# A recurrence with routed experts: a block reordered, transposed keys moved into A's PSUM banks, routing spread over four blocks

## Chip, cores and metric

The kernel runs on 1 core of one Trainium2 chip. The metric is device time in microseconds (us) of that core. Engines are named as in the profile: PE (TensorE; its weight loads are PEld), DVE (VectorE), ACT (ScalarE), POOL (GpSimd) and SP (SyncE, which here only issues DMAs).

## What is computed

The reference is a linear recurrence over time for 4 batches and 8 heads of width 48, and a top-1 mixture of experts behind it:

```
for t in range(768):                                   # per batch and head
    cur   = outer(u * k[t], v[t])
    y[t]  = r[t] @ (state + cur)
    state = w[t][:, None] * state + outer(k[t], v[t])
x = y as 3072 tokens of 384
logits = x @ w_gate; e = argmax(logits); gate = softmax(logits)[e]
out = gate * (relu(x @ w1[e]) @ w2[e])                 # 8 experts, 384 -> 1024 -> 384
```

## The kernel before

**Recurrence.** Time is cut into 24 blocks n = 0..23 (12 chunks of 64 steps, two batch pairs), so blocks n and n+2 belong to one recurrence and n%2 says which. For a block the kernel makes, on DVE, running products of w from the front (`pre`, L322, with the reciprocal of their ends, L325) and from the back (`suf`, L331); kh = k * suf on DVE (`dve_kh`, L339); rh = r * pre and rk = r * k on POOL (`pool_rh` L364, `pool_rk` L358). On PE: the transposed keys (`pe_kt`, four transposes, L465), the 64 by 64 products A = kh x rh (`pe_a`, 32 matmuls, L418), the part of the output that comes from the state (`pe_inter`, 32 matmuls, L435), the part inside the block (`pe_av`, 32 matmuls, L444), the new state U (`pe_dp`, 32 matmuls, L456), the u-coefficients (`pe_c`, 16 matmuls, L476) and the transposed output xT (`pe_xT`, 3 transposes, L484). ACT copies PSUM to SBUF: kt (L396), g from U (L377), ct (L382), xr from yp (L404), xT (L409); it also writes the diagonals of the matrix `at`, eight activations a block (`act_diag`, L390), and two small paddings (`act_pad` L368, `act_pend` L372). DVE then copies the lower half of A over `at` under a mask (`dve_at`, L344), and `pe_av` multiplies `at` by v. `zeros` (L123) issues matmuls by a tile of zeros whose results nobody reads: three of 504 columns with the coefficients and six of 256 columns after A (more in the first blocks).

**Routing.** Every fourth block the previous group of four (G = n // 4 - 1) is routed in one go: logits (`logit_mm`), a transpose (`logit_tr`), `gate` on DVE and ACT, `rank` on PE, `weigh` and `place` on DVE. Then each block's 128 rows go to the table `xs` in DRAM by an indirect DMA from POOL (`scatter`, L556), one block per iteration. After group FIRST = 3 the kernel picks the first expert (`choose`), and `feed` starts to load its weights; `side` splits a loaded third of a piece into a high and a low part, an activation on ACT (L213) and a subtraction on DVE (L215).

**Order.** Every engine runs its instructions in the order in which `iteration` issues them, all written by hand; semaphores are placed automatically. PSUM has eight banks: one for `cell`, two each for U, A (`ap`) and the output (`yp`), and one, `psM`, which kt, ct, xT, logits and rank take in turn, each waiting until the one before was read. In an iteration PE runs kt(n), AV(n), zeros and c(n+2), dp(n), inter(n+1), A(n+1), xT(n), zeros. Each iteration also loads block n+6 on SP's queue (`load`, `load_v`). From n = 18 on, an iteration ends with a `side`, and three more run after block 22 (L754 to L774).

**Experts.** Behind block 23 PE transposes the rows of the first expert, `mm1` multiplies by w1 (L282) and `contract` by w2 (L295), expert after expert, with weights split beside it.

Of the kernel before, what the change touches and what calls it, by code (L numbers as in the profile page):

```python
# [19 lines left out]
P = 128  # L20
C = 64
# [31 lines left out]
def rwkv_moe_kernel(ctx, tc, rkw, vv, ub, wg, wr, w1, w2, out):  # L53
# [357 lines left out]
    def pe_a(n):  # L411
        if real(n):
            d = blk[n]
            d["ap"] = ap = psA.tile([P, 2, BANK], F32, name="ap", tag="ap")
            for q in range(NQ):
                for b in range(2):
                    for j in range(2):
                        nc.tensor.matmul(ap[half(b), j, q * C:(q + 1) * C], d["kh"][part(j), 2 * q + b, :],  # L418
                                         d["rh"][part(j), 2 * q + b, :], start=True, stop=True, skip_group_check=True)

    def pe_fill(n):
        if real(n):
            for i in range(6 if n > 4 else 16):
                zeros(blk[n]["ap"][:, i % 2, NQ * C:], 1)

    def pe_inter(n):
        if real(n):
# [10 lines left out]
    def pe_av(n):  # L438
        if real(n):
            d = blk[n]  # L440
            for q in range(NQ):
                for b in range(2):
                    for j in range(2):
                        nc.tensor.matmul(d["yp"][half(b), j, q * D:(q + 1) * D], d["at"][half(b ^ j), j, q, :],  # L444
                                         d["v"][half(b ^ j), (j * NQ + q) * D:(j * NQ + q + 1) * D],
                                         start=(n < 2 and q == 0), stop=(q == NQ - 1), skip_group_check=True)

    def pe_dp(n):
        if real(n) and n < NB - 2:
# [8 lines left out]
                                         start=(n == 0 and q == 0), stop=True, skip_group_check=True)  # L458

    def pe_kt(n):  # L460
        if real(n) and n < NB - 2:
            d = blk[n]
            d["kp"] = psM.tile([P, BANK], F32, name="kp", tag="m")[:, 0:NQ * RP]
            for q in range(NQ):
                nc.tensor.transpose(d["kp"][:, q * RP:(q + 1) * RP], d["kh"][:, 2 * q:2 * q + 2, :].rearrange("p b c -> p (b c)"),  # L465
                                    ident[:RP, :RP])

    def pe_c(n):
        if real(n):
            d = blk[n]  # L470
            t = psM.tile([P, BANK], F32, name="cp", tag="m")
            d["cp"] = cp = t[:, 0:H]
            zeros(t[:, H:], 8 if n < 4 else 3)
# [5 lines left out]
    def pe_xT(n):  # L479
        if real(n):  # L480
            G, i = divmod(n, GRP)
            blk[n]["xp"] = xp = psM.tile([P, BANK], F32, name="xp", tag="m")[:, 0:DM]
# [17 lines left out]
    def logit_few(k):  # L500
        G, i, m = k
        lt = psM.tile([P, BANK], F32, name="lt", tag="m")[:, 0:m * E].rearrange("p (b e) -> p b e", e=E)
# [19 lines left out]
    def rank(k):  # L522
        G, i, m = k
        oh = ch["r", k][0]
        rk = psM.tile([P, BANK], F32, name="rank", tag="m")[:, 0:(m + 1) * E].rearrange("p (b e) -> p b e", e=E)
# [7 lines left out]
        nc.scalar.activation(nb, rk[0:1, m, :], AF.Copy)  # L533

    def place(k):
        G, i, m = k
# [107 lines left out]
    def iteration(n):  # L644
# [3 lines left out]
        if n >= 0:  # L648
            load(n + 6)
            load_v(n + 6)  # L650
        route = 0 <= g < NG - 1
        act_g(n + 1)
        if route and i == 0:
            scatter(g - 1, (3,)) if g > 0 else None
        if route and i > 0:
            scatter(g, (i - 1,))
        pe_kt(n)
        dve_at(n)
        act_kt(n)
        dve_pre(n + 2)  # L660
        act_pend(n + 2)
        pe_av(n)
        act_xr(n)
        pool_rk(n + 3)
        pe_c(n + 2)
        act_ct(n + 2)
        dve_suf(n + 2)
        pool_rh(n + 2)
        if n == 0:
            pass  # L670
        act_diag(n + 2, range(0, 4))
        pe_dp(n)
        dve_scale(n + 2)
        pe_inter(n + 1)
        pe_a(n + 1)
        pe_xT(n)
        pe_fill(n + 1)
        act_xT(n)
        act_diag(n + 2, range(4, 8))
        act_pad(n + 4)  # L680
        dve_kh(n + 2)
        if route and i == 0:
            logit_mm(g)
            logit_tr(g)
            gate(whole)
            pool_ids(g)
            rank(whole)
            weigh(whole)
            place(whole)
        if n == 0:  # L690
            zero_rows()
        if n == 1:
# [58 lines left out]
    with tc.manual_schedule(engines={ET.PE, ET.DVE, ET.Activation, ET.Pool}):  # L751
        last = NG - 1
        ka, kb = (last, 0, 2), (last, 2, 2)
        for n in range(-3, NB):  # L754
            iteration(n)
            if n == FIRST * GRP + GRP:
                choose()
                eid[0] = expert_of(first[0:1, 0:1])
                feed()
            if n == FIRST * GRP + 2 * GRP:  # L760
                ua = rows_of(HA, 0, 0)
            if n == NB - 3:
                side()
            if n == NB - 2:
                logit_few(ka)
                gate(ka)
                rank(ka)
                side()
                weigh(ka)
                place(ka)  # L770
                for i in range(3):
                    side()
# [8 lines left out]
        scatter(last - 1, (3,))  # L781
        pool_ids(last)
        scatter(last, (0, 1))
        for j in range(3):
# [317 lines left out]
```

## Time and profile before

| what | value |
|---|---|
| median of 3 runs | 475.72 us (472.07 to 476.95) |
| the profiled execution: its time | 479.51 us |
| its span, first to last instruction | 477.7 us |
| PE busy | 419.9 us (88% of the span) |
| DVE, ACT, POOL busy | 259.8, 215.5, 133.1 us |
| mean granted PE clock | 0.906 of 2.4 GHz |
| DMA, mean over the span | 143 GB/s |

A timeline row is: start in us, length in us, engine, line, operation, out<-in, count, and in brackets how long the engine had been idle before it and what ended that. A row of several instructions merges neighbours. A row of a table by stretch is: stretch, its length, then busy us and count of PE, PEld, DVE, ACT, POOL, then PE's granted clock, the share of the DMA engines, and GB/s.

### The profile page before, as it was taken

Reading aid. Unit: us, or ns where it says so; the run is one execution under the profiler, and the core shown is the slowest. Engines: PE = TensorE matmul, PEld = TensorE weight load, DVE = VectorE, ACT = ScalarE, POOL = GpSimd, SP = SyncE. Lnnn points to the kernel's source line nnn. Section 1 sums busy time; section 2 is a strip of 40 time slices with the busy share of each in tenths; the row PEclk is TensorE's granted clock in tenths of the full one; section 3 lists DMA queues with packets and bytes.
Section 4 is the critical chain, followed back from the end, with each engine's and each line's share of the span. In section 5 each row is a group of like instructions: output and inputs, shape, how many; then the busy total and the mean of one; then the engine's idle time right before and its main releaser. Section 6 shows DMA issues by size and latency. Waiting matters only on the chain. (4 is left out here: it accounts for less than half of the span.)

```text
span 477.7 us, 13153 instructions
## 1 busy us (share of the span) xinstructions
PE 419.9 (88%) x5416; PEld 371.4 (78%) x5416; DVE 259.8 (54%) x447; ACT 215.5 (45%) x584; POOL 133.1 (28%) x162
## 2 busy tenths in 40 slices
PE   8999898888987787648989999999999999699991
PEld 5667576665765556547979999999999999699990
DVE  7357686556575554232455463664647553475472
ACT  1556465456455544332244452553626342263461
POOL 4543246552644441210120100402104052102121
PEclk9999899799699967565889999999999999799996
DMA  8966767334363711200198254344564625555341
GB/s 226 258 172 170 196 186 213 108 109 140 104 173 94 250 52 33 101 18 18 60 269 294 69 179 138 101 153 137 164 183 118 191 68 166 163 145 190 105 142 44
DMA packets 39236, 68.09 MB, mean 143 GB/s; under 512 B 8692, under 2 KB 21573, under 8 KB 39170
## 3 DMA queue, kind: packets, MB, share of 16 engines
q1 hardware_dynamic: 32050, 57.68, 41.7%
q0 software_dynamic: 7120, 9.51, 6.3%
q8 instruction: 44, 0.72, 0.6%
q14 instruction: 22, 0.18, 0.1%
HBM read 55.30 MB, written 12.04 MB: 141 GB/s over the span
## 5 line engine op out<-in xcount | busy, mean ns | idle before, releaser
L246 POOL DMA_INDIRECT out_dram<-ot,xg x16 | 24.3, 1520 | 104.7 <-DVE ot L869 101.0
L390 ACT ACTIVATE at<-id,ct 128x64 f32<-128x64 f32 x192 | 50.6, 336 | 0.8
L556 POOL DMA_INDIRECT xs<-xr,pi x24 | 25.6, 1067 | 77.8 <-DVE w2l L215 17.2
L123 PEld LDWEIGHTS <-ones 128*128 128x128 bf16 x350 | 34.7, 107 | 16.0 <-issue 3.2
L215 DVE TENSOR_TENSOR w1l<-wst,w1h 128x512 fp32r<-128x512 f32 x48 | 33.1, 690 | 24.5 <-ACT w1h L213 24.4
L246 POOL DMA_INDIRECT out_dram<-ort,xg x13 | 17.9, 1380 | 91.6 <-DVE ort L300 68.2
L364 POOL TENSOR_TENSOR rh<-rkwt,pre 112x512 f32<-112x512 f32 x24 | 28.4, 1185 | 52.8 <-DVE pre L322 40.9
L444 PE MATMUL yp<-vt,at 64*64 64x48 f32 x768 | 19.1, 245 | 20.7 <-DVE at L344 20.0
L215 DVE TENSOR_TENSOR w2l<-wst,w2h 128x512 fp32r<-128x512 f32 x48 | 32.0, 689 | 9.2 <-ACT w2h L213 8.9
L295 PE MATMUL N<-w2h,hh 128*126 128x384 f32 (+4 forms) x104 | 36.6, 352 | 0.3 <-DVE ort L300 0.3
L444 PEld LDWEIGHTS yp<-vt,at 64*64 64x64 f32 x768 | 15.9, 157 | 26.1 <-DVE at L344 25.3
L344 DVE COPY_PREDICATED at<-cmask,ap 128x512 f32<-128x512 int32 x24 | 17.4, 723 | 34.4 <-PE ap L123 34.4
L295 PE MATMUL N<-w2h,hl 128*126 128x384 f32 (+4 forms) x104 | 35.8, 344 | 0.0
L295 PE MATMUL N<-w2l,hh 128*126 128x384 f32 (+4 forms) x104 | 35.7, 344 | 0.0
L285 DVE SCALAR_TENSOR_TENSOR hl<-N,hh 128x256 fp32r<-128x256 f32 (+8 forms) x37 | 19.3, 525 | 27.5 <-ACT hh L284 27.5
L358 POOL TENSOR_TENSOR rk<-rkwt 112x512 f32<-112x512 f32 x24 | 30.9, 1288 | 8.4 <-DMA rkwt<-in_rkw_dram 8.4
L213 ACT ACTIVATE w1h<-wst 128x512 fp32r<-128x512 f32 x48 | 29.8, 624 | 6.6 <-DMA wst<-in_w_dram 6.6
L331 DVE TENSOR_TENSOR_SCAN suf<-rkwt,cell 112x536 f32<-112x536 f32 x24 | 30.5, 1271 | 0.8
L322 DVE TENSOR_TENSOR_SCAN pre<-rkwt,cell 112x536 f32<-112x536 f32 x24 | 30.1, 1255 | 1.1 <-DMA rkwt<-in_rkw_dram 1.1
L213 ACT ACTIVATE w2h<-wst 128x512 fp32r<-128x512 f32 x48 | 28.4, 623 | 2.8 <-DMA wst<-in_w_dram 2.8
L409 ACT ACTIVATE xT<-xp 128x384 f32<-128x384 f32 x24 | 11.8, 490 | 38.9 <-PE xp L484 38.9
L282 PE MATMUL N<-xh,w1h 128*128 128x440 f32 (+6 forms) x84 | 28.8, 343 | 0.0
(178 smaller groups left out, 1076.1 us busy)
## 6 DMA issues: line engine op xcount, KB each, us to landing
wst<-in_w_dram SPq DMA_DIRECT2D x48, 256.0 KB
wst<-in_w_dram SPq DMA_DIRECT2D x16, 768.0 KB
rkwt<-in_rkw_dram SPq DMA_DIRECT2D x72, 96.0 KB
rkwt<-in_rkw_dram SPq DMA_DIRECT2D x24, 238.0 KB
vt<-in_vv_dram SPq DMA_DIRECT2D x24, 192.0 KB
wck_t<-in_wr_dram SPq DMA_DIRECT2D x6, 768.0 KB
rkwt<-in_rkw_dram SPq DMA_DIRECT2D x12, 224.0 KB
xs<-zrow SPq DMA_DIRECT2D x8, 289.5 KB
```

What stands on the lines that cost most here:

```text
L123: nc.tensor.matmul(t, ones, wz[:, 0:t.shape[1]], start=True, stop=True, skip_group_check=True)
L213: nc.scalar.activation(hi, st[:, cs], AF.Copy)
L215: nc.vector.tensor_tensor(out=lo, in0=st[:, cs], in1=hi.bitcast(F32), op=ALU.subtract)
L246: i = nc.gpsimd.indirect_dma_start(out=out[:, :], out_offset=bass.IndirectOffsetOnAxis(ap=t.bitcast(I32)[:, q, DM + 1:DM + 2], axis=0), in ...
L282: nc.tensor.matmul(hp, a, x[p][:, j, :], start=(i == 0), stop=(i == 8))
L295: nc.tensor.matmul(op, a[:, cs], w2v(wt, w, f), start=(i == 0), stop=(i == 23))
L322: nc.vector.tensor_tensor_scan(out=d["pt"][:, 0, 0:NW], data0=d["w"], data1=cell[:RP, 0:1].broadcast_to([RP, NW]), initial=1.0, op0=ALU.mu ...
L331: nc.vector.tensor_tensor_scan(out=suf[:, ::-1], data0=d["w"][:, ::-1], data1=cell[:RP, 0:1].broadcast_to([RP, NW]), initial=1.0, op0=ALU. ...
L358: nc.gpsimd.tensor_tensor(out=d["rk"], in0=d["r"], in1=d["k"], op=ALU.mult)
L364: nc.gpsimd.tensor_tensor(out=d["rh"], in0=d["r"], in1=d["pre"][:, :, 1:C + 1], op=ALU.mult)
L390: nc.scalar.activation(d["at"][:, h // NQ, h % NQ, :], id2, AF.Copy, scale=d["ct"][:, h:h + 1])
L444: nc.tensor.matmul(d["yp"][half(b), j, q * D:(q + 1) * D], d["at"][half(b ^ j), j, q, :], d["v"][half(b ^ j), (j * NQ + q) * D:(j * NQ + q ...
```

## The change

A block's work now lies in one iteration: kt(n), inter(n), A(n), then the copy into `at`, then xT(n-1), c(n+2) and zeros in one bank, AV(n), dp(n). suf, rh, kh and the diagonals are made one block ahead instead of two. The transposed keys get no bank of their own: they go into the 256 columns of A's two banks that A leaves free. xT and the coefficients share one tile of `psM`, with zeros in its last 120 columns (six, or sixteen in the first blocks); `pe_fill` is gone. Routing is spread: logits at i = 0 of the four blocks, transpose and ids at i = 1, `gate`, `rank` and `weigh` at i = 2, `place` at i = 3, the scatters from i = 3 to i = 2 of the next four. The first expert is chosen after block 19 instead of 16; two `side`s remain inside the loop, after blocks 22 and 23.

```diff
 def act_kt(n):
-            nc.scalar.activation(d["kt"], d["kp"], AF.Copy)
+            nc.scalar.activation(d["kt"].rearrange("p (j c) -> p j c", j=2), d["ap"][:, :, NQ * C:NQ * C + 2 * RP], AF.Copy)
-    def pe_fill(n):
-        if real(n):
-            for i in range(6 if n > 4 else 16):
-                zeros(blk[n]["ap"][:, i % 2, NQ * C:], 1)
 def pe_kt(n):
+        if real(n):
+            blk[n]["ap"] = psA.tile([P, 2, BANK], F32, name="ap", tag="ap")
-            d["kp"] = psM.tile([P, BANK], F32, name="kp", tag="m")[:, 0:NQ * RP]
             for q in range(NQ):
+                o = NQ * C + (q % 2) * RP
+                nc.tensor.transpose(d["ap"][:, q // 2, o:o + RP], ...)
+    def pe_xc(n):
+        t = psM.tile([P, BANK], F32, name="xc", tag="m")
+        pe_xT(n - 1, t)
+        pe_c(n + 2, t)
+        zeros(t[:, DM + H:], 16 if n < 4 else 6)
 def iteration(n):
+        pe_kt(n)
+        pe_inter(n)
+        pe_a(n)
+        if full and i == 2:
+            gate(whole)
+        if full and i == 3:
+            place(whole)
+        dve_scale(n + 1)
+        dve_suf(n + 1)
+        pool_rh(n + 1)
+        dve_kh(n + 1)
+        act_kt(n)
         act_g(n + 1)
+        act_diag(n + 1, range(8))
         dve_at(n)
+        if full and i == 3:
+            scatter(g, (0, 1) if g == FIRST else (0,))
+        if g > 0 and i < 3 and g - 1 != FIRST:
+            scatter(g - 1, (i + 1,))
+        if g - 1 == FIRST and i == 0:
+            scatter(FIRST, (2, 3))
+        pool_rk(n + 3)
+        pe_xc(n)
         dve_pre(n + 2)
+        act_xT(n - 1)
+        act_ct(n + 2)
         pe_av(n)
         act_xr(n)
+        act_pend(n + 2)
+        act_pad(n + 4)
+        if full and i == 2:
+            weigh(whole)
         pe_dp(n)
+        if full and i == 0:
             logit_mm(g)
+        if full and i == 1:
             logit_tr(g)
             pool_ids(g)
+        if full and i == 2:
+            t = rank(whole)
+            if n == NB - 2:
+                logit_few((NG - 1, 0, 2), t)
 for n in range(-3, NB):
+            if n == NB - 1:
+                gate(ka)
             iteration(n)
-            if n == FIRST * GRP + GRP:
+            if n == FIRST * GRP + 7:
                 choose()
...
-            if n > FIRST * GRP + GRP + 1:
                 side()
+        scatter(last - 1, (1, 2, 3))
+        t = psM.tile([P, BANK], F32, name="xc", tag="m")
+        pe_xT(NB - 1, t)
+        act_xT(NB - 1)
```

## Rows read from the trace of the kernel before

**Rows 1.** Table by stretch: five stretches of the recurrence, one block each
```profile
64.10:69.80 5.70, 5.23 (x160) 4.10 (x160) 4.54 (x7) 3.89 (x14) 1.41 (x3) 1.00 0.75 185
...
102.00:108.80 6.80, 5.82 (x160) 4.46 (x160) 4.03 (x6) 3.93 (x16) 3.52 (x4) 1.00 0.54 168
108.80:117.80 9.00, 7.05 (x192) 5.35 (x192) 5.14 (x12) 5.49 (x20) 1.32 (x2) 1.00 0.48 134
117.80:127.50 9.70, 9.37 (x160) 7.17 (x161) 4.95 (x6) 4.16 (x15) 6.10 (x7) 0.51 0.42 123
...
201.80:214.60 12.80, 6.62 (x126) 5.90 (x126) 4.59 (x12) 3.96 (x9) 2.04 (x3) 0.63 0.05 16
```

**Rows 2.** Timeline of PE, block 7 at full clock
```profile
64.07 0.68 PE L444 MATMUL yp<-vt,at 64*64 64x48 f32 x32 [0.29 <-DVE at L344]
64.92 0.80 PE L123 MATMUL cp<-wz,ones 128*128 128x504 bf16 x3 [0.17 <-ACT kt L396]
65.65 0.64 PE L476 MATMUL cp<-ubt,rk 112*64 112x8 f32 x16
66.22 0.62 PE L456 MATMUL U<-vt,kt 64*64 64x48 f32 x30
...
67.77 0.55 PE L484 MATMUL xp<-ident,xr 128*128 128x128 f32 x3
68.16 0.82 PE L123 MATMUL ap<-wz,ones 128*128 128x256 bf16 x6
```

**Rows 3.** Timeline of DVE: what released the copy into at, and place
```profile
46.90 0.73 DVE L344 COPY_PREDICATED at<-cmask,ap 128x512 f32<-128x512 int32 x1 [1.67 <-PE ap L123]
...
56.29 0.19 DVE L539 TENSOR_TENSOR ps<-rank,oh 128x32 f32<-128x32 f32 x1 [0.49 <-ACT base L533]
```

**Rows 4.** Timeline of ACT: the copies and diagonals of a block
```profile
13.55 2.02 ACT L390 ACTIVATE at<-id,ct 128x64 f32<-128x64 f32 x8
...
100.46 0.49 ACT L409 ACTIVATE xT<-xp 128x384 f32<-128x384 f32 x1 [1.85 <-PE xp L484]
...
101.91 0.47 ACT L377 ACTIVATE g<-U 112x384 f32<-112x384 f32 x1
...
102.28 0.53 ACT L396 ACTIVATE kt<-kp 128x448 f32<-128x448 f32 x1
...
104.28 0.18 ACT L382 ACTIVATE ct<-cp 128x8 f32<-128x8 f32 x1 [1.07 <-PE cp L476]
```

**Rows 5.** Groups by line, first 250 us: line, engine, tiles, count | busy us, mean ns
```profile
L331 DVE TENSOR_TENSOR_SCAN suf<-rkwt,cell 112x536 f32<-112x536 f32 x24 | 30.5, 1271 | 0.8
...
L215 DVE TENSOR_TENSOR w1l<-wst,w1h 128x512 fp32r<-128x512 f32 x12 | 8.2, 689 | 24.5 <-ACT w1h L213 24.4
```

**Rows 6.** Timeline of POOL and DVE near 60 us
```profile
59.40 1.27 POOL L358 TENSOR_TENSOR rk<-rkwt 112x512 f32<-112x512 f32 x1
60.63 1.19 POOL L364 TENSOR_TENSOR rh<-rkwt,pre 112x512 f32<-112x512 f32 x1
...
60.12 2.26 DVE L339 TENSOR_TENSOR kh<-rkwt,suf 112x512 f32<-112x512 f32 x1
```

**Rows 7.** Timeline of POOL and PE near 105 us: a scatter and inter
```profile
104.55 1.01 POOL L556 DMA_INDIRECT xs<-xr,pi  x1 [0.15 <-ACT ct L382]
...
105.84 0.47 PE L435 MATMUL yp<-g,rh 64*64 64x48 f32 x15 [0.40 <-issue]
```

**Rows 8.** Timeline of POOL: two blocks that waited for their loads
```profile
13.03 1.26 POOL L358 TENSOR_TENSOR rk<-rkwt 112x512 f32<-112x512 f32 x1 [1.10 <-DMA rkwt<-in_rkw_dram]
...
16.52 1.27 POOL L358 TENSOR_TENSOR rk<-rkwt 112x512 f32<-112x512 f32 x1 [1.08 <-DMA rkwt<-in_rkw_dram]
```

**Rows 9.** Timeline of PE: first and last AV, first contraction of an expert
```profile
19.39 0.68 PE L444 MATMUL yp<-vt,at 64*64 64x48 f32 x32 [0.53 <-DVE at L344]
...
214.56 1.10 PE L444 MATMUL yp<-vt,at 64*64 64x48 f32 x32 [4.91 <-DVE at L344]
...
235.35 0.34 PE L295 MATMUL N<-w2h,hh 128*128 128x384 f32 x1
```

More of the change, by code (lines that the diff above doesn't have):

```diff
@@ L413, in pe_a @@
             d = blk[n]
-            d["ap"] = ap = psA.tile([P, 2, BANK], F32, name="ap", tag="ap")
+            ap = d["ap"]
             for q in range(NQ):
@@ L444, in pe_av @@
                         nc.tensor.matmul(d["yp"][half(b), j, q * D:(q + 1) * D], d["at"][half(b ^ j), j, q, :],
-                                         d["v"][half(b ^ j), (j * NQ + q) * D:(j * NQ + q + 1) * D],
-                                         start=(n < 2 and q == 0), stop=(q == NQ - 1), skip_group_check=True)
+                                             d["v"][half(b ^ j), (j * NQ + q) * D:(j * NQ + q + 1) * D],
+                                             start=(n < 2 and q == 0), stop=(q == NQ - 1), skip_group_check=True)
     def pe_dp(n):
@@ L460, in pe_kt, with pe_c @@
     def pe_kt(n):
+        if real(n):
+            blk[n]["ap"] = psA.tile([P, 2, BANK], F32, name="ap", tag="ap")
         if real(n) and n < NB - 2:
             d = blk[n]
-            d["kp"] = psM.tile([P, BANK], F32, name="kp", tag="m")[:, 0:NQ * RP]
             for q in range(NQ):
-                nc.tensor.transpose(d["kp"][:, q * RP:(q + 1) * RP], d["kh"][:, 2 * q:2 * q + 2, :].rearrange("p b c -> p (b c)"),
+                o = NQ * C + (q % 2) * RP
+                nc.tensor.transpose(d["ap"][:, q // 2, o:o + RP], d["kh"][:, 2 * q:2 * q + 2, :].rearrange("p b c -> p (b c)"),
                                     ident[:RP, :RP])
-    def pe_c(n):
+    def pe_xc(n):
[3 more added lines that the diff above has]
+        zeros(t[:, DM + H:], 16 if n < 4 else 6)
+    def pe_c(n, t):
         if real(n):
             d = blk[n]
-            t = psM.tile([P, BANK], F32, name="cp", tag="m")
-            d["cp"] = cp = t[:, 0:H]
-            zeros(t[:, H:], 8 if n < 4 else 3)
+            d["cp"] = cp = t[:, DM:DM + H]
             for q in range(NQ):
@@ L477, in pe_c, with pe_xT @@
                                      skip_group_check=True)
-    def pe_xT(n):
+    def pe_xT(n, t):
         if real(n):
             G, i = divmod(n, GRP)
-            blk[n]["xp"] = xp = psM.tile([P, BANK], F32, name="xp", tag="m")[:, 0:DM]
+            blk[n]["xp"] = xp = t[:, 0:DM]
             for j in range(3):
@@ L498, in logit_tr, with logit_few @@
         ch["lp", (G, 0, GRP)] = lt[:, 0:P].rearrange("p (b e) -> p b e", e=32)[:, :, 0:E]
[L500 removed]
+    def logit_few(k, t=None):
         G, i, m = k
[L502 removed]
+        t = psM.tile([P, BANK], F32, name="lt", tag="m") if t is None else t[:, BANK // 2:BANK]
+        lt = t[:, 0:m * E].rearrange("p (b e) -> p b e", e=E)
         for b in range(m):
@@ L524, in rank @@
         oh = ch["r", k][0]
-        rk = psM.tile([P, BANK], F32, name="rank", tag="m")[:, 0:(m + 1) * E].rearrange("p (b e) -> p b e", e=E)
+        t = psM.tile([P, BANK], F32, name="rank", tag="m")
+        rk = t[:, 0:(m + 1) * E].rearrange("p (b e) -> p b e", e=E)
         ch["rank", k] = rk
@@ L650, in iteration @@
             load_v(n + 6)
-        route = 0 <= g < NG - 1
-        act_g(n + 1)
[L653 to L657, printed above, removed]
-        dve_at(n)
-        act_kt(n)
+        full = 0 <= g < NG - 1
+        pe_kt(n)
[10 more added lines that the diff above has]
+        act_kt(n)
+        act_g(n + 1)
+        act_diag(n + 1, range(8))
+        dve_at(n)
+        if full and i == 3:
[6 more added lines that the diff above has]
+        pe_xc(n)
         dve_pre(n + 2)
-        act_pend(n + 2)
+        act_xT(n - 1)
+        act_ct(n + 2)
         pe_av(n)
         act_xr(n)
[L664 to L671, printed above, removed]
-        pe_dp(n)
[L673 to L682, printed above, removed]
+        act_pend(n + 2)
+        act_pad(n + 4)
+        if full and i == 2:
+            weigh(whole)
+        pe_dp(n)
+        if full and i == 0:
             logit_mm(g)
+        if full and i == 1:
             logit_tr(g)
-            gate(whole)
             pool_ids(g)
-            rank(whole)
-            weigh(whole)
-            place(whole)
+        if full and i == 2:
+            t = rank(whole)
+            if n == NB - 2:
+                logit_few((NG - 1, 0, 2), t)
         if n == 0:
@@ L759, in rwkv_moe_kernel @@
                 feed()
-            if n == FIRST * GRP + 2 * GRP:
+            if n == FIRST * GRP + 8:
                 ua = rows_of(HA, 0, 0)
-            if n == NB - 3:
+            if n == NB - 2:
                 side()
-            if n == NB - 2:
-                logit_few(ka)
-                gate(ka)
+            if n == NB - 1:
                 rank(ka)
-                side()
                 weigh(ka)
                 place(ka)
-                for i in range(3):
-                    side()
-            if n > FIRST * GRP + GRP + 1:
                 side()
+        scatter(last - 1, (1, 2, 3))
+        t = psM.tile([P, BANK], F32, name="xc", tag="m")
+        pe_xT(NB - 1, t)
+        act_xT(NB - 1)
         pctx.close()
@@ L780, in rwkv_moe_kernel @@
         bk["c"] = N[4:6]
-        scatter(last - 1, (3,))
         pool_ids(last)
```

1 line of the change is left out of this document (added).

## The prediction

> **What bounds the kernel now.** I read the table by stretch first, one block of the recurrence per row, then the timelines of PE, ACT and DVE inside a block, then the waits. The first AV starts at 19.39 us, the last at 214.56, and the first `contract` at 235.35 [rows 9]: 23 gaps of 8.5 us on average, 41% of the span, and a PE that is nearly full behind them. So what the recurrence gives up comes off the end, since the expert phase follows on PE.
>
> A quiet block takes 5.7 us, one with a scatter 6.8, one that routes 9.0, the one after it 9.7 because PE runs at 1.2 GHz (granted 0.51 after a stretch of 7.05 busy of 9.0), and the last ones up to 12.8 [rows 1]. The quiet block is one chain: the fill after A holds the banks that the copy into `at` reads, the copy then sits between fill and AV (PE idle 0.29), AV goes on to coefficients, dp, inter, A, xT and fill [rows 2]. A routing block adds logits, transpose, gate, rank and place in series, PE idle between each. In the last five blocks a weight split sits on ACT and DVE ahead of `at`; AV of block 23 came after 4.91 us of idle PE [rows 9].
>
> **The change part by part.**
>
> *PE's own work.* AV 0.6; c 0.57 (65.65 to 66.22); dp, inter and A together 1.55 (66.22 to 67.77), so about 0.5 each with A the longest; xT 0.39; kt four transposes at xT's rate, 0.5 [rows 2]. Fill: six times 120 columns instead of 3x504 and 6x256. From 0.82 for 6x256 [rows 2] that is 0.4, at least 0.2, at most the same 0.8. Sum 4.0 us.
>
> *DVE's work.* `at` 0.62 to the next start (0.73 less overlap [rows 3]), suf and pre 1.29 each from 1.27 [rows 5], the reciprocal 0.3, kh. kh shows 2.26 us where POOL ran rk and then rh, ending 0.57 after POOL did [rows 6]; freed of POOL I take 0.7. In the new order rh runs during suf and rk behind it, so kh can meet rk: 0.7 to 1.7; I take 1.2, as a scatter lies between the two in most blocks. Sum 4.7 (4.2 to 5.2). The Trainium skill ("SBUF — State Buffer", section "Who interferes with whom") says that a VectorE instruction with two inputs in SBUF and a GpSimd instruction that reads SBUF exclude each other, and the later one waits for the whole other. By that rule kh costs 1.7 in each block without a scatter between rh and rk; the row agrees in that kh waited for two POOL instructions in turn. Without it DVE's sum would be 4.2. Neither passes ACT's loop below in a quiet block; it adds in the block with `gate`.
>
> *Who waits for whom.* Does the copy of kt wait for A, which is in other columns of the same banks? Two rows say yes: the copy into `at` was released by the fill, whose columns it does not read, and `place` by ACT's copy of `base`, two reads of one bank [rows 3]. So I take dependences by bank: kt's copy waits for A(n), `at`(n) for kt's copy, xT's copy and ct for the last zeros. Chain on DVE and PE: A's end, kt copy 0.6, `at` 0.8 with signals, AV 0.6, dp 0.5, kt 0.5, inter 0.5, A 0.7 to its end: 4.2. xT, c and zeros (1.36) about cover the two copies (1.4), so this loop is bound by neither alone.
>
> *ACT's loop is longer.* ACT goes in order: kt, g, eight diagonals, xT, ct, xr; inter(n+1) needs xr's copy, as `yp` has one buffer; then A(n+1), then kt's copy. From A's end: signal 0.05; kt 0.44; g 0.37 (101.91 to 102.28); diagonals 1.93 (2.02 less the overlap); xT 0.39; ct 0.2; xr 0.49, the same shape as xT [rows 4]; signal 0.06; inter 0.47; A 0.7. Sum 5.1 us. Behind xr on ACT stands only a padding of 0.1. POOL: rh 1.2, rk 1.25 [rows 6], scatter 1.0 with its memset and gaps 1.3 [rows 7]: 3.8. Loads: about 3.5 us a block (two waits for loads, 13.03 and 16.52 [rows 8]). So a quiet block takes 5.1, set by ACT.
>
> *Routing, spread.* Logits cannot start before ct is read, 3.4 us after A's end, take 0.85 and push kt and inter past xr: +0.8. The transpose: +0.2. `gate`, three DVE operations of 0.2 ahead of suf, and rank on PE: +0.8. `place`: +0.2. Two us a group instead of the 3.3 (9.0 against 5.7) and the clock's fall after it [rows 1]; from 1 to 3. `choose` 0.9 once.
>
> *Scatters.* Inter lasted about 1 us longer where a scatter ended on POOL: PE stood for "issue" until 105.84, when the scatter of 104.55 was just over [rows 7]. This explains 6.8 against 5.7 [rows 1]. It is moved against PE's order: where it falls into AV or dp, ACT's loop hides it; where into inter or A, it costs 1. Half: 17 times 0.5 = 8.5, from 0 to 17.
>
> *Queues that the steps pass.* On POOL the scatter now stands between rh(n+1) and rk(n+3), so a scatter that waits (for `place`, or for prefilled rows to land) holds rk, which PE wants one block later, and then rh(n+2), which inter wants: 2 us of slack a block (3.8 of 5.9). On DVE `gate` and `place` stand ahead of suf and kh, and so of `at`: counted above. On ACT the diagonals stand between kt and xT, ct, xr: that is the loop. On SP the first weights are asked for behind the last load, with the queue empty; the expert's rows follow them, and wait for the same scatters as before.
>
> *Splits.* Nine of eleven leave the loop. Four remain ahead of the first `mm1`, three of which stand in front of its last products at 0.7 on DVE [rows 5]: +2 behind block 23. Weights are asked for three blocks later, with three blocks left: hidden; if not, the same +2 grows to some 5.
>
> *Clock.* PE is busy 4.0 of 5.1, and in routed blocks 4.8 of 6 with weak spots together. It fell to 1.2 GHz after the routing block [rows 1]. I put in two falls at 2 us: 4.
>
> *Sum.* First AV at 18 (kh and suf of block 1 now go ahead of `at`, but the long fills go; 19.39 before [rows 9], which is the upper end, 17 the lower); 23 x 5.1 = 117; routing 5 x 2.0 = 10; `choose` 1; scatters 8.5; clock 4; the last two blocks, without kt and dp, -1.5. Last AV at 157 against 214.56. Profiled execution: 479.5 - 214.6 + 157 + 2 = 424. It was 3.8 above the median of the runs, so 420 there (-12%).
>
> **Rivals**, in times on the median's footing.
>
> *The clock gives way* (24%). Without the big fills PE's pattern may be too thin. For it: the fall above; against it: quiet blocks held 1.00 with PE busy 5.82 of 6.8 [rows 1], though with 1.5 us of fill in them. At 1.2 GHz the block after routing had PE busy 9.37 [rows 1]; less twice the two old fills (2 x 1.5) and with the new one at 0.8 that is 7.2, with waits 7.9, against 5.9 on average above. Half the blocks so: +23, 443.
>
> *Slower, one mechanism* (6%): the clock stays at 1.2 GHz for the whole recurrence. Block 7.9, routing at that clock +0.7 on average, scatters +0.4: 9.0; last AV at 20 + 23 x 9.0 = 227: 490. It decides from 8.4 us a block on; below, the change is still a gain. For it: in the last block before the granted mean was 0.63 with PE busy 6.62 of 12.8 [rows 1]. Against: there PE was idle in stretches near 5 us, which the new order has not.
>
> *Loads bind* (10%). 3.5 us a block is under 5.1, but the table's prefill (eight writes) and scatters share the queues in blocks 2 to 9. Each of some ten blocks 1 us late: 430.
>
> *No wait by bank* (8%). The Trainium skill ("PSUM — Partial Sum Buffer", section "PSUM bank collisions raise a hardware error") wants engines kept apart by bank and quadrant, not by address. By that rule the time is my 420. If the kernel waited by address, kt's copy would start before inter and leave ACT's loop free by 1.2 us; DVE would set 4.5 a block: 23 x 0.6 less, 405.
>
> *The change does not do what it says* (2%): kt's copy or the shared tile is serialized so that the quiet block stays at 5.7 and routing at 3.3 a group; only the splits' 20 us go: 455.
>
> **How the numbers follow.** Forecast 50%, its own range 405 to 434 (routing and scatters at their ends, zero to four falls). With the rivals' 405, 430 and 443 inside, the range is 403 to 446; it leaves out the 490, the 455 and part of the clock's tail. A measurement here can tell about 1% from no change. Faster by over 1%: 0.92 (all but the slow case and the last of the clock's); within 1%: 0.02; slower: 0.06.
>
> **What would show it.** Right: quiet blocks of 5.1 to 5.3 us with inter released by ACT's xr; kt's copy released by A; `at` by ACT's kt; blocks with logits near 6; no idle PE over 1.5 us before AV; about 2 us more between the last AV and the first `contract`. Wrong: granted clock near 0.5 over many blocks, PE's gaps ended by `at`, POOL or DVE waiting for rkwt's loads, kh near 1.7 with AV released by `at` each time, or a wait for the weights behind block 23.

## The result and the profile after

The changed kernel takes 433.33 us in the median of four runs (430.38 to 436.17), the kernel before 476.34 in its four beside them (472.07 to 479.47): a ratio of 0.912, interval 0.903 to 0.922. Measured once more (f_after below) the ratio was 0.909 (0.902 to 0.916). Ratios and their intervals leave out executions more than 1.5% above the fastest of their kernel. The forecast of 420 had the direction and most of the size; the time lies 13 us above it, inside the range.

The profiled execution took 432.83 us (span 431.0), against 479.51 of before. Where the gain sits is read from the same three rows of PE's timeline as in [rows 9], with one quiet block between them, PE and ACT and DVE together:

```profile
17.48 0.69 PE L439 MATMUL yp<-vt,at 64*64 64x48 f32 x29
...
35.30 0.68 PE L439 MATMUL yp<-vt,at 64*64 64x48 f32 x32
36.56 0.49 ACT L404 ACTIVATE xr<-yp 128x384 f32<-128x384 f32 x1
36.67 0.43 PE L451 MATMUL U<-vt,kt 64*48 64x48 f32 x14 [0.36 <-issue]
37.57 0.68 PE L430 MATMUL yp<-g,rh 64*64 64x48 f32 x32
38.80 0.54 ACT L396 ACTIVATE kt<-ap 128x448 f32<-128x448 f32 x1 [1.65 <-PE ap L418]
39.38 0.73 DVE L344 COPY_PREDICATED at<-cmask,ap 128x512 f32<-128x512 int32 x1 [0.40 <-ACT kt L396]
40.16 0.55 PE L439 MATMUL yp<-vt,at 64*64 64x48 f32 x20
...
165.02 1.11 PE L439 MATMUL yp<-vt,at 64*64 64x48 f32 x32
...
186.77 0.34 PE L295 MATMUL N<-w2h,hh 128*128 128x384 f32 x1
```

From first to last AV it is now 147.5 us, where it was 195.2: 47.6 us less, and the end of the kernel is 46.7 us earlier. The last AV to the first `contract` takes 21.75 us (20.79 before), and what is behind that, to the end of the execution, 246.1 (244.2). So the recurrence gave everything, as the forecast said, and nearly all of it reached the end.

The table by stretch of the same kernel, first the whole recurrence, then single blocks from AV to AV (columns as in [rows 1]: length, busy us and count of PE, PEld, DVE, ACT, POOL, granted clock, DMA share, GB/s):

```profile
17.48:165.02 147.54, 123.12 (x3711) 104.33 (x3710) 112.54 (x155) 88.50 (x330) 74.19 (x104) 0.87 0.60 170
35.30:40.16 4.86, 4.50 (x159) 3.79 (x157) 4.36 (x6) 3.21 (x13) 2.42 (x2) 1.00 0.85 204
...
82.89:90.57 7.68, 5.05 (x164) 4.25 (x164) 6.14 (x9) 5.12 (x21) 3.51 (x4) 1.00 0.48 145
114.07:121.31 7.24, 7.24 (x158) 6.21 (x158) 6.46 (x7) 3.48 (x14) 3.54 (x4) 0.50 0.50 148
...
127.36:133.56 6.20, 4.43 (x160) 3.74 (x159) 5.14 (x9) 4.99 (x21) 3.56 (x4) 1.00 0.44 134
138.49:146.57 8.08, 4.30 (x157) 3.64 (x158) 7.91 (x11) 5.49 (x22) 6.46 (x9) 1.00 0.44 134
```

A quiet block takes 4.9 us. The others carry something each: `place` (82.89), the clock at its lower level, 1.2 GHz, with PE without a gap (114.07), `choose` (138.49). How much of the recurrence ran at 1.2 GHz follows from a row: a mean of 0.87 over 147.54 us is 2 x 0.13 x 147.54 = 38 us.

What PE did in the recurrence changed in one term above all. The first row is the whole recurrence of the kernel before; the other two hold only `zeros` (L123), so only PE and PEld, in the kernel before and in the changed one:

```profile
19.39:214.56 195.17, 158.86 (x3817) 122.32 (x3817) 111.91 (x166) 100.15 (x337) 79.70 (x112) 0.86 0.47 135
```
```profile
19.39:214.56 195.17, 48.42 (x254) 25.12 (x254) 0.86 0.47 135
```
```profile
17.48:165.02 147.54, 13.71 (x169) 9.94 (x168) 0.87 0.60 170
```

PE was busy 35.7 us less (158.86 to 123.12), and 34.7 of that are zeros (48.42 to 13.71); all its other matmuls took 110.4 and 109.4 us. The rest is waiting: PE's waits add up to 36.6 us before and 23.9 after. In the kernel before, the zeros stood in the chain of a block [rows 2, rows 3], so the smaller fill alone may have given much of the gain. No run has the old order with the smaller fill, so how much stays open; k_two below has the small fill and is slower than the kernel before, so it isn't enough in every order. The first row also says that the kernel before ran 2 x 0.14 x 195.17 = 55 us at 1.2 GHz, more than the 38 of the changed one.

The waits of the same stretch (engine, line, waited for: us in total, times, longest), PE's, then ACT's and DVE's:

```profile
PE yp L439 <- DVE at L344: 13.0, 10, 3.2
PE yp L439 <- issue: 3.5, 2, 2.0
```
```profile
ACT kt L396 <- PE ap L418: 35.9, 21, 3.1
```
```profile
DVE at L344 <- ACT kt L396: 17.5, 8, 4.5
```

AV waits for `at` as before, 13.0 us (20.0 in the kernel before), and for nothing else as long. A second profile of the same program, f_after below, has 6.2, so a fall from 13.0 to about 6 tells nothing by itself. `at` is late for two reasons that can be told apart. One is the bank: `at` is held by ACT's copy of kt, which itself stood for A, whose columns it doesn't read. The other is `place`. The timeline of its block in the changed kernel:

```profile
85.56 0.17 ACT L536 ACTIVATE base<-rank 1x8 f32<-1x8 f32 x1 [0.97 <-PE rank L533]
85.77 0.19 DVE L543 TENSOR_TENSOR ps<-rank,oh 128x32 f32<-128x32 f32 x1 [1.44 <-ACT base L536]
86.09 1.26 DVE L331 TENSOR_TENSOR_SCAN suf<-rkwt,cell 112x536 f32<-112x536 f32 x1
86.99 1.01 POOL L560 DMA_INDIRECT xs<-xr,pi  x1 [1.67 <-DMA vt<-in_vv_dram]
87.39 2.50 DVE L339 TENSOR_TENSOR kh<-rkwt,suf 112x512 f32<-112x512 f32 x1
88.06 1.27 POOL L358 TENSOR_TENSOR rk<-rkwt 112x512 f32<-112x512 f32 x1
89.81 0.71 DVE L344 COPY_PREDICATED at<-cmask,ap 128x512 f32<-128x512 int32 x1
90.57 0.62 PE L439 MATMUL yp<-vt,at 64*64 64x48 f32 x28 [1.99 <-DVE at L344]
```

`place` (L543) is first in DVE's block, and waits 1.44 us for ACT's read of the same bank; suf and kh come late by that; kh then meets GpSimd's rk and takes 2.50 us in place of 0.69; `at` and AV wait in turn.

### The profile page after: what moved, and what is told of

The parts are those of the page before. It is cut to its first block, busy times and chain, and to the rows that moved or that the text cites. A ratio compares the mean times of both kernels' runs of the same rounds, so it can differ in the third digit from the quotient of the medians.

```text
span 431.0 us, 13044 instructions
## 1 busy us (share of the span) xinstructions
PE 386.1 (90%) x5361; PEld 356.6 (83%) x5362; DVE 265.2 (62%) x447; ACT 208.0 (48%) x584; POOL 132.5 (31%) x162
## 5 line engine op out<-in xcount | busy, mean ns | idle before, releaser
L246 POOL DMA_INDIRECT out_dram<-ot,xg x16 | 24.3, 1521 | 104.7 <-DVE ot L876 101.0
L390 ACT ACTIVATE at<-id,ct 128x64 f32<-128x64 f32 x192 | 48.2, 340 | 0.0
L560 POOL DMA_INDIRECT xs<-xr,pi x24 | 24.2, 1010 | 26.0 <-issue 10.5
L344 DVE COPY_PREDICATED at<-cmask,ap 128x512 f32<-128x512 int32 x24 | 17.4, 724 | 23.6 <-ACT kt L396 22.5
L339 DVE TENSOR_TENSOR kh<-rkwt,suf 112x512 f32<-112x512 f32 x24 | 30.7, 1279 | 0.8
L213 ACT ACTIVATE w2h<-wst 128x512 fp32r<-128x512 f32 x48 | 28.7, 624 | 3.0 <-DMA wst<-in_w_dram 3.0
L396 ACT ACTIVATE kt<-ap 128x448 f32<-128x448 f32 x22 | 12.0, 544 | 36.5 <-PE ap L418 36.5
L273 DVE TENSOR_TENSOR xl<-N,xh 128x440 fp32r<-128x440 f32 (+6 forms) x21 | 11.9, 565 | 28.7 <-ACT xh L272 28.7
```

The lines of the kernel that those rows point to most:

```text
L213: nc.scalar.activation(hi, st[:, cs], AF.Copy)
L246: i = nc.gpsimd.indirect_dma_start(out=out[:, :], out_offset=bass.IndirectOffsetOnAxis(ap=t.bitcast(I32)[:, q, DM + 1:DM + 2], axis=0), in ...
L339: nc.vector.tensor_tensor(out=d["kh"], in0=d["k"], in1=d["suf"][:, :, 3:SEG], op=ALU.mult)
L390: nc.scalar.activation(d["at"][:, h // NQ, h % NQ, :], id2, AF.Copy, scale=d["ct"][:, h:h + 1])
L560: i = nc.gpsimd.indirect_dma_start(out=xsf, out_offset=bass.IndirectOffsetOnAxis(ap=ch["pi", G, b], axis=0), in_=xr[:, b, :], in_offset=No ...
```

## The experiments

The runs were made in three groups of four, each with the kernel before beside it: its median was 482.04, 482.57 and 484.19 us there. Ratios are to these.

**a_splits: only the splits leave the loop.** The kernel before, with the first `side` behind block 22:

```diff
-            if n == NB - 3:
-                side()
...
-            if n > FIRST * GRP + GRP + 1:
+            if n >= NB - 2:
                 side()
```

> The kernel before, with nothing of the new order: only the weight splits are moved out of the loop (one after block 22, one after block 23, the rest behind the loop). Theory: in the last five blocks the split stood on ACT and DVE ahead of the copy into at, so they fall from 57 us to some 36 and 2 to 3 come back behind the loop: about 458. Rival: the splits have to be done anyway, and the stretch before the first contraction takes them back: 470 to 476.

472.01 us, ratio 0.977 (0.970 to 0.984): 11 us, or 465 on the footing of 476, between the two. In its profile the last AV started at 204.96 and the first `contract` at 228.40, so 9.6 us came out of the recurrence and 2.6 went into the tail. Its last three blocks still took 9.4, 11.5 and 10.0 us: the splits were not all that made the last blocks of [rows 1] long.

**b_route1: routing of a group in one block.** The changed kernel with `logit_mm`, `logit_tr`, `gate`, `rank`, `weigh`, `place` together at i = 0, and the scatters where the kernel before has them, one block behind:

```diff
-        if full and i == 2:
-            gate(whole)
-        if full and i == 3:
-            place(whole)
...
         if full and i == 0:
             logit_mm(g)
+            logit_tr(g)
+            gate(whole)
+            pool_ids(g)
+            rank(whole)
+            weigh(whole)
+            place(whole)
```

> The changed kernel with the routing of a group in one block again (logits, transpose, gate, rank, weigh and place in series at i = 0, scatters as in the kernel before). Theory: spreading is worth the difference between the old series (3.3 us a group and a fall of the clock, 2 to 3 more) and what the spread routing costs now (about 3.9 a group over quiet blocks): some +8 to +12, 443. Rival: with place at the head of a DVE block the spread routing costs as much as the series: 433 within 4.

452.22 us (445.81 to 453.6), with no interval on record. The two executions that count, 445.81 and 450.99 us, are 0.925 and 0.936 of the kernel before, the changed kernel 0.909 to 0.912. So the spreading, scatters included, is worth some 0.013 to 0.027 of the time before: 6 to 13 us, or 1.3 to 2.6 for each of five groups. PE's waits in its recurrence:

```profile
PE yp L439 <- DVE at L344: 8.6, 8, 2.1
PE xc L477 <- POOL rk L358: 7.6, 2, 3.8
```

AV's 8.6 us for `at` lie between the two profiles of the changed kernel. The second row is what the prediction named under the queues: a scatter that waits on POOL holds rk behind it, and PE's coefficients with it. Here it happened twice, so these 7.6 us belong to the place of the scatters and not to the series of steps.

**c_place: `place` behind suf and kh.** One of the two causes of the late `at` alone:

```diff
-        if full and i == 3:
-            place(whole)
         dve_scale(n + 1)
         dve_suf(n + 1)
         pool_rh(n + 1)
         dve_kh(n + 1)
+        if full and i == 3:
+            place(whole)
```

> The changed kernel with place moved behind suf and kh on DVE (still ahead of the copy into at). Theory: place waits at the head of DVE's block for ACT's copy of base, which stands behind rank at the end of PE's block; suf, kh and at then run late, and kh meets POOL's rk: about 2 us in each of four or five blocks. So about 424, AV no longer waiting 1.3 to 2.5 us in blocks 7, 11 and 15. Rival: those blocks are held by PE's order or ACT's loop as well, and give back less than 3 us: 431 to 433.

434.28 us, ratio 0.903 (0.896 to 0.910). DVE's wait of `place` for `base` is gone (4.1 us in the changed kernel's profile, 5.9 in f_after), as the theory says; the time hardly moved. PE's waits of its recurrence:

```profile
PE ap L418 <- issue: 4.5, 9, 1.7
PE yp L439 <- DVE at L344: 3.3, 6, 1.2
```

9.7 us less for `at` (13.0 to 3.3), 5.1 us more of "issue", in which PE has its operands and issues nothing (all such rows: 5.5 us in the changed kernel's profile, 10.6 here). Part of either may be no work of the edit: f_after has 6.2 and 10.6 without one.

**d_atfirst: the copy of kt behind `at`.** The other cause alone:

```diff
-        act_kt(n)
         act_g(n + 1)
         act_diag(n + 1, range(8))
         dve_at(n)
+        act_kt(n)
```

> The changed kernel with ACT's order turned: g and the eight diagonals first, then kt's copy, and the copy into at issued ahead of kt's copy (so at waits for A alone, kt's copy for at). Theory of the prediction: ACT's loop sets the quiet block at 5.1, with ACT idle 1.3 to 1.7 us for A in it; filling that idle time shortens quiet blocks to 4.5 to 4.7: 424 to 428. Rival: the quiet block is PE's own stream with its issue waits and the routed ones are DVE's, so nothing moves: 431 to 435.

433.83 us, ratio 0.899 (0.893 to 0.905). The order of the waits turned: `at` is now released by A (18.3 us in 8 waits) and no longer by the copy of kt. But AV's wait for `at`, 7.3 us, is not below the 6.2 of f_after, the rows of "issue" are 13.6, and the time is below the changed kernel's by no more than the intervals leave open. The theory, that ACT's idle time holds the quiet block, isn't borne out.

**f_after, e_both: the changed kernel again, and both moves in one.** The edit of e_both is that of c_place and d_atfirst together.

> The changed kernel itself, once more, as the base of the runs beside it. Both theories expect a ratio to the kernel before of 0.91 (its first measurement gave 0.9124). What it tells apart: in the two runs with an earlier PLACE or AT the tail began with some 4 us in which ScalarE stood before the last copy of xr and TensorE before the last transposes (169.39 us of the run with PLACE moved). If that stop belongs to those two orders, this run doesn't have it (the first profile of the changed kernel had 0.5 us there); if it belongs to the execution, it can show here too.

> The changed kernel with both moves of the earlier runs: PLACE behind SUF and KH on VectorE, and ScalarE's copy of kt behind AT. Theory: the waits of AV for AT (13.0 us in the changed kernel's profile, 3.3 with the first move alone, 7.3 with the second alone) come from two separate causes, PLACE at the head of VectorE's block and the read of one bank by two engines; with both moves under 3 us stay, and the time is 8 to 10 us below the changed kernel's. Rival: TensorE, at 4.96 us of matmuls a block and with stops in which it has no instruction to issue (10 to 13 us in each of the two), is now the bound; then both moves give no more than one of them, 4 to 7 us, and the stops grow.

f_after: 440.66 us, ratio 0.909 (0.902 to 0.916). e_both: 432.83, ratio 0.899 (0.894 to 0.904). e_both has the lowest median of all, and by its ratio it is 10% below the kernel before, no more than d_atfirst alone. Its six executions (428.14 to 433.56) all lie below the four of the changed kernel beside it (437.08 to 443.74): 1.8% by the medians, 1.1% by the ratios, whose intervals overlap a little. The rival is nearer: with both moves AV still waits 5.0 us for `at`, and the stops without an instruction, 13.3 us, are as long as with either move alone (10.6 and 13.6). PE's waits in the recurrence of e_both:

```profile
PE ap L418 <- issue: 5.2, 9, 2.4
PE yp L439 <- DVE at L344: 5.0, 6, 2.0
PE yp L439 <- issue: 4.5, 5, 2.8
```

f_after answers two questions. It has the stop ahead of the last copy of xr too (3.3 us in ACT's waits, put to none of the core's engines), so that stop is not of c_place's and d_atfirst's orders; the profiles of e_both, g_nofill, j_keys, l_rk and i_choose have it too, with 3.0 to 4.3 us. The first profile of the changed kernel and that of b_route1 are the exceptions. And it is the same program as the changed kernel in a second profile, with a longer recurrence. Its waits and its table by stretch:

```profile
PE yp L439 <- DVE at L344: 6.2, 8, 1.7
PE ap L418 <- issue: 5.7, 7, 2.5
```
```profile
18.50:174.97 156.47, 134.29 (x3711) 113.00 (x3710) 111.19 (x155) 88.55 (x330) 74.19 (x103) 0.80 0.56 159
```

8.9 us more than the 147.54 above, with a granted mean of 0.80 against 0.87: 2 x 0.20 x 156.47 = 63 us at 1.2 GHz against 38. PE was busy 134.29 us there against 123.12, and its waits were 2.3 us shorter, so the difference lies in the busy time. The two were taken in different groups, and the kernel before was 6 us slower beside the second too. So one program differs between two executions by more than any of these moves gives, and the clock moves with it.

**g_nofill, h_fill12: no zeros from block 4 on, and twelve instead of six.**

```diff
-        zeros(t[:, DM + H:], 16 if n < 4 else 6)
+        zeros(t[:, DM + H:], 16 if n < 4 else 0)
```

> The changed kernel without the six matmuls of zeros in the blocks from 4 on (0.49 us a block by the profile of the changed kernel). Theory: the blocks that wait for nothing (4.9 to 5.4 us) are bound by TensorE itself, whose matmuls sum to 4.96 us a block at full clock, so each such block, some ten of them, gives 0.5 us and the kernel 3 to 6 us (ratio to the unchanged order about 0.99, some 428 against 433); the blocks that wait for AT give nothing. Rival: the zeros keep the clock up, and without them the granted clock falls more often or longer, which costs 2 to 5 us a fall; then the time stays or rises by up to 10 us, and the mean granted clock is below the 0.913 of the changed kernel's profile.

> The changed kernel with twelve matmuls of zeros in place of six in the blocks from 4 on (0.49 us more a block). Theory that TensorE bounds the blocks which wait for nothing: 3 to 6 us longer, some 438 against 433. Rival that the clock is what the zeros are worth: fewer of the five falls, so up to 5 us shorter, with a mean granted clock above 0.913.

444.48 us, ratio 0.919 (0.912 to 0.927), and 439.23, ratio 0.909 (0.904 to 0.915); the changed kernel beside them 440.66. The mean granted clock of the timed executions was 0.857 to 0.877 without zeros, 0.887 to 0.917 with six and 0.916 to 0.930 with twelve: the zeros do hold the clock up. But neither edit moved the time by what a measurement tells. The table by stretch of g_nofill:

```profile
18.13:175.06 156.93, 132.04 (x3591) 111.59 (x3590) 109.66 (x155) 88.30 (x331) 73.62 (x103) 0.75 0.55 158
```

78 us at 1.2 GHz (2 x 0.25 x 156.93), 16 more than f_after, in a recurrence of the same length: 120 zeros fewer are some 10 us at 0.49 for six, but PE was busy only 2.3 us less than in f_after. What was saved on zeros went to the clock, and to waits (24.3 us against 21.6). Both expectations have an error of mine: "4.96 us of matmuls a block" adds the rows' lengths, which overlap. A block in which PE ran from AV to AV without a gap at full clock, from 90.57 to 94.85 in the changed kernel's profile, took 4.28 us, zeros included.

**j_keys, k_two: two parts of the change undone.** The transposed keys in a tile of their own from the one-bank ring; and xT and the coefficients in two tiles of that ring:

```diff
+            d["kp"] = psM.tile([P, BANK], F32, name="kp", tag="m")[:, 0:NQ * RP]
             for q in range(NQ):
-                nc.tensor.transpose(d["ap"][:, q // 2, o:o + RP], ...)
+                nc.tensor.transpose(d["kp"][:, q * RP:(q + 1) * RP], ...)
```
```diff
     def pe_xc(n):
         t = psM.tile([P, BANK], F32, name="xc", tag="m")
         pe_xT(n - 1, t)
+        t = psM.tile([P, BANK], F32, name="cc", tag="m")
         pe_c(n + 2, t)
```

> The changed kernel with one part undone: the transposed keys go to a tile of their own from the ring of one bank (with xT, the coefficients and the routing), not to the spare columns of A's banks. Theory, by the sum of the prediction: each block's key transposes then wait for ScalarE's copy of ct out of that bank, which ends 0.6 to 0.8 us after TensorE could go on (the routing's tiles in the same bank wait 0.6 to 0.8 us each for it in the changed kernel's profile); 23 blocks by 0.6 are 14 us, less the 5 us or so that AT gains because ScalarE's copy of kt no longer waits for A: 8 to 10 us longer than the changed kernel, ratio to before about 0.93. Rival: the copy of kt does not hold AT any more and the transposes find ScalarE done in the blocks that are slow anyway, so that the time is that of the run with kt's copy behind AT, ratio 0.90.

> The changed kernel with another part undone: xT and the coefficients in two tiles, one after the other, from the ring of one bank. Theory: TensorE's coefficient matmuls wait until ScalarE has copied xT, which in the changed order stands behind g and the eight diagonals (2.5 us); in a quiet block of the changed kernel's profile the transposes of xr end at 137.26 us and the copy of xT at 140.18, so TensorE stands some 2 us a block, of which AV's wait for AT takes back a part: 1 to 1.5 us by 23, 23 to 35 us longer (ratio 0.96 to 0.98). Rival: AV waits for AT anyway, and the coefficients are needed two blocks later; then under 8 us longer (ratio under 0.925).

j_keys: 438.92 us, ratio 0.908 (0.892 to 0.923). The theory is wrong in its place: the key transposes never waited for ct, only for the routing's tiles (7.1 us in 13 waits, all in routed blocks), and AV's wait for `at` was 4.1 us. What released `at` shows the wait by bank most plainly: with kt in another bank and ACT's order unchanged, its copy no longer holds `at` in any block, and only A does:

```profile
DVE at L344 <- PE ap L418: 21.6, 12, 3.6
```

The time can't be told from the changed kernel's, so the spare columns of A's banks, taken alone, brought nothing measurable.

k_two: 519.98 us, ratio 1.077 (1.065 to 1.088), slower than the kernel before. Its timeline, its waits in the recurrence and its table by stretch:

```profile
106.17 1.03 PE L478 MATMUL cc<-ubt,rk 112*64 112x8 f32 x16 [2.94 <-ACT xT L409]
```
```profile
PE cc L478 <- ACT xT L409: 60.4, 21, 3.4
```
```profile
18.41:248.95 230.54, 166.24 (x3711) 142.26 (x3710) 107.40 (x155) 92.64 (x331) 74.83 (x104) 0.63 0.38 109
```

The place was as expected, the size not: 2.9 us a block where 2 were expected, and a clock of 0.63 over the recurrence (170 us at 1.2 GHz), which the expectation left out. The recurrence is 83 us longer than the changed kernel's: all of PE's waits together are 40.4 us longer (64.3 against 23.9, as the 60.4 of this wait took the place of others, AV's for `at` among them), and PE was busy 43.1 us longer with the same matmuls (166.24 against 123.12), which goes with the low clock. So the new order, with xT's copy behind eight diagonals on ACT, pays only because xT and the coefficients share a bank.

**l_rk, i_choose: GpSimd's rk one block later and ahead of rh; the choice behind kh.** Both on e_both:

```diff
+        if n >= 3:
+            pool_rk(n + 2)
         pool_rh(n + 1)
...
-        pool_rk(n + 3)
+        if n < 2:
+            pool_rk(n + 3)
```
```diff
+        if n == FIRST * GRP + 8:
+            choose()
         dve_at(n)
```

> The kernel with both moves (PLACE behind SUF and KH, kt's copy behind AT), and from block 3 on GpSimd multiplies rk of block n+2 ahead of rh of block n+1, where it was rk of n+3 behind rh and the scatter. In that kernel's profile 22 KH take 24.7 us between 18 and 165 us, 1.12 each, where one alone takes 0.69: 9.5 us in which VectorE stands, by the records beside it while GpSimd scatters and multiplies rk. Theory: with rk beside the scan of pre, only the scatter can still meet KH; its mean falls to 0.8 and the kernel is 3 to 6 us shorter than with both moves alone (ratio 0.887 to 0.893). Rival: it is the scatter that holds KH, or the wait moves to rh (GpSimd is late for inter): ratio 0.899 or above, KH still over 1.0.

> The kernel with both moves, and the choice of the first expert emitted one block later, behind KH and ahead of AT, where it was behind the scan of pre of block 19. Theory: its first instruction, 1x8, took 1.77 us in the changed kernel's profile and 2.92 with PLACE moved, both while GpSimd multiplied rk and rh; in the new place GpSimd scatters, it takes under 0.5 us, and the block of the choice falls from 8.2 us to some 6: 2 us less, ratio 0.895. Rival: the instruction meets rk in the new place too and holds AT, which AV waits for directly: no gain, ratio 0.899 to 0.905.

l_rk: 435.12 us, ratio 0.906 (0.895 to 0.916). The experiment was badly built: rk ahead of the next rh is, on an engine that runs in order, where rk behind the scatter already was. So l_rk has e_both's order on POOL and is nearly e_both measured once more. In its profile kh still meets rk (81.34 and 81.46 below), and 22 kh took 21.6 us, 0.98 each.

```profile
81.34 1.28 POOL L358 TENSOR_TENSOR rk<-rkwt 112x512 f32<-112x512 f32 x1
...
81.46 1.73 DVE L339 TENSOR_TENSOR kh<-rkwt,suf 112x512 f32<-112x512 f32 x1
```

i_choose: 435.27 us, ratio 0.906 (0.895 to 0.916). The instruction is cured (0.15 us below, while a scatter ran; 2.92 in c_place's profile, the second fence), the time not.

```profile
138.42 0.15 DVE L569 SCALAR_TENSOR_TENSOR key<-base,kofs 1x8 f32<-1x8 f32 x1
```
```profile
137.51 2.92 DVE L569 SCALAR_TENSOR_TENSOR key<-base,kofs 1x8 f32<-1x8 f32 x1
```

Neither beats e_both. With 0.906 for both, e_both's own gain over the changed kernel (0.909 to 0.912) may be smaller than the 0.899 says.

## Why the prediction was right, and where its sum was off

**What bounds it, and what follows.** Right. The recurrence gave 47.6 us, and the expert phase followed.

**Quiet block, 5.1 us.** Right in size (4.86 and 5.08 us in two that waited for little), but not shown for the reason given. ACT's loop should have released inter through xr; in the block above xr had ended at 37.05, inter came at 37.57 behind PE's own transposes, and ACT then stood 1.65 us for A. ACT's loop (5.1 by the prediction's terms), PE (4.28 without a gap) and DVE (4.36 busy in that block) lie close together, and none is shown to be alone the bound.

**Dependences by bank.** Right: the rows of kt and `at` above show it, and j_keys shows it from the other side: with kt in another bank its copy never held `at`. The rival without a wait by bank is out. (Its 405 would be 406 by its own figures, and its 4.5 for DVE is not the 4.7 of the sum.) Two reads of one bank also set the wait of `place`.

**The fill.** The forecast counted the smaller fill in PE's own work, and then took ACT as the bound of the quiet block, so it never said what the fill is worth. In PE's account it is 34.7 of the 47.6 us; no run tells what it would have given in the old order.

**Routing, 2 us a group.** Its largest error is `place`, put at 0.2: it waits 1.44 us for ACT's copy of `base`, at the head of DVE's block, and the block's AV was 1.99 us late. c_place took those waits out and gave at most about 1%, within the intervals: the term was mis-sized, yet it isn't what the time is short of. Spreading, with the scatters' place, gave 6 to 13 us by b_route1; the forecast had 1.3 a group and the clock's fall after it.

**Scatters, 8.5 us.** The mechanism fell. PE's stop for "issue" at inter under a scatter is not in the changed kernel's profile (no such row at L430). Stops without an instruction do add up to 5.5 us there and 10.6 in f_after, but nearly all at AV, U and A; f_after has one at inter, 1.2 us, which ended 0.6 us behind a scatter. On DVE kh took 1.30 us a block (28.7 us for 22), near the 1.2 taken, but by another mix than the forecast's. A scatter between rh and rk shields kh only in part: five kh beside a scatter alone took 0.69 us, but five that met the scatter and the rk right behind it took 2.1 to 2.5; the seven that met rk alone took 1.4 to 1.6, the other five 0.69. That the mean came out is in part luck.

**Clock, two falls, 4 us.** This is the term that failed most. The profile had 38 us at 1.2 GHz. Two executions of one program give a price: 24 us more at the low level (62.6 against 38.4) went with 8.9 us more of recurrence, 0.37 each, so 38 cost some 14; this is an estimate from a pair that differs in other waits too. A lower estimate is the block at 114.07, 7.24 at 0.50 against 6.20 at full clock in the block at 127.36: 5 us. Either way the term is 1 to 10 us short; the recurrence as a whole was 8.5 us longer than the 139 forecast. "The clock gives way" was the rival with the most weight, and the time lies between it and the forecast; but against the kernel before, with its 55 us at 1.2 GHz, the clock did not give way.

**Tail, +2.** +1.0 to `contract`, +1.9 behind it. With first and last AV (17.48 for 18, 165.02 for 157) this closes the sum: -0.5 + 8.5 - 1.0 + 1.9 = 8.9, and 432.83 - 424 = 8.8. On the median's footing the gap is 13 us: the profiled execution was 3.8 above the median before and 0.5 below it after. That the sum comes so near is in part luck: the 8.5 us for scatters stand for a stop that hardly occurred, while the clock and `place` took more than their terms.

**The signs.** Of the signs of being right, the copy of kt released by A and a longer tail came, and `at` was held by ACT's kt in 8 blocks; idle PE before AV reached 3.2 us where 1.5 was the limit. Of the signs of being wrong one came: PE's waits were ended by `at` more than by anything else, 13.0 of 23.9 us. Loads did not bind: rk on POOL waited 2.2 us for them in the whole recurrence.

**Splits, 20 us in the rival's price.** 11, by a_splits. The parts measured apart are 11 for the splits and 6 to 13 for the spread routing; some 19 to 26 remain for the order with its shared bank and the smaller fill, which no run separates. These are differences between different kernels and needn't add.

## What to carry to other kernels

When three engines each fill most of a block, the waits move: in c_place, d_atfirst and e_both AV waited 3.3 to 7.3 us for `at`, in two profiles of the unchanged program 13.0 and 6.2, and all of PE's waits in the recurrence together were 20 to 24 us in all five. Take a second profile of the same program before a per cent is explained. Add up an engine's busy time by line before and after: here that points to the zeros, which no experiment had isolated. And when an order is changed, look at which buffers the old order shared for free: one bank for two tiles was worth more here than the whole change.

## What the runs showed of the hardware that was not expected

**A small instruction of DVE can stand for microseconds.** One with 1x8 operands took 2.92 us in c_place, and ended with GpSimd's rk and rh; kh at 87.39 started 0.67 us ahead of rk, no more than its own length of 0.69, and still stood until rk was over. The Trainium skill ("SBUF — State Buffer", section "Who interferes with whom") says that the ports the two share are an exclusive lock, and that issue order decides who blocks. By that rule kh should have ended first; here it started first in the records and ended last. A scatter alone doesn't hold either of them: in the changed kernel five kh beside one took 0.69 us (the first at 74.03), and in i_choose the 1x8 instruction took 0.15. Starts on POOL are rough, and what held the two here stays open.

**PE stops without an instruction, for longer in the shorter recurrences.** In the four kernels with the longest (168 to 231 us: b_route1, a_splits, before, k_two) the rows of "issue" add up to 2.3 to 6.2 us, in the ten profiles of 140 to 157 us to 5.5 to 15.4, without a strict order among these. Two of the longest stops began close to a packet of the instruction queue. PE's timeline in e_both, and the queue between 23.2 and 23.6 us (packets, MB, share of the engines):

```profile
23.01 0.31 PE L439 MATMUL yp<-vt,at 64*64 64x48 f32 x2
26.13 0.62 PE L439 MATMUL yp<-vt,at 64*64 64x48 f32 x27 [2.81 <-issue]
```
```profile
q1 hardware_dynamic: 56, 0.09, 108.3%
q8 instruction: 1, 0.02, 20.9%
```

The load queue is full in the same 0.4 us. In the changed kernel a stop of 1.49 us ahead of 42.21 followed such a packet at 39.6. But 30 such packets lie in e_both's 139.81 us, one every 4.7 us, so one nearby is weak evidence. That PE waits for its own code behind the loads is argued from this, not shown; no run moved the loads. The Trainium skill ("Runtime: NRT & Kernel Launch", section "Instruction fetch mechanics") says that engines fetch code by a DMA queue of their own in blocks of 16 KiB, and that crossing into the next is mostly hidden. The size agrees (44 packets with 0.72 MB in all in the changed kernel); that it is hidden would not fit stops of 1.5 to 2.8 us, if these are its cause. The 3 to 4 us in which ACT stood ahead of the last xr may be of the same kind; that too is open.
